# Turning the tails of the attention outputs: fp32 products and a split behind them, or a split ahead and fp16 products

## The chip, the cores and the metric

The kernel runs on one core of a Trainium2 chip. The metric is the device time of one execution in microseconds. One execution was recorded by the hardware profiler; times of the profile are counted from its first instruction. The engines are TensorE (PE, with its weight loads PEld), VectorE (DVE), ScalarE (ACT), GpSimd (POOL) and SyncE (SP, which here issues all DMAs).

## The reference, cut to what matters

```python
# q, k, v: (8 batches, 8 heads, 1152, 64), float32
q_pool = q.reshape(B, H, S // 2, 2, D).mean(axis=3)             # 576 query rows
scores = 1 / sqrt(D) * matmul(q_pool, k.transpose(0, 1, 3, 2))
attn = softmax(scores, axis=-1)
x = matmul(attn, v)  ->  (8, 576, 512), heads side by side
# gated unit
h = maximum(x @ w_in, 0);  u, v = h[..., :512], h[..., 512:]
v_n = (v - mean) / sqrt(var + 1e-6)                             # over the 512 columns
v_s = einsum('ts,bsd->btd', w_spatial, v_n) + b_spatial[None, :, None]
out = (u * v_s) @ w_out
```

All of it is wanted in float32. The kernel reaches that with fp16 products by splitting an operand into two fp16 parts, head and rest, and adding three of the four partial products.

## The kernel before, in words

The work is cut into 32 head pairs i (8 batches of 4 pairs; a pair is two heads in one 128-partition tile). `attention(i)` runs 18 steps, 2 heads by 9 chunks of 128 keys. Each step makes a tile of scores for 512 query rows (L1076, L1077, in a bank `pss`, three of them), takes the exponential on ACT (L1082, tile `pt`), splits it on POOL (L1102) and multiplies it with the split values (L977, L983, L988, into the bank `o`). The query rows number 576 per head, so 64 are left over, the *tail*. The tails of the two heads are done together: scores L1089 and L1093, exponential L1098, and `tail_values(i)` (L1046 to L1048), whose result, divided by its sum, L1052 writes to the tile `xt`. `xt` is [128, 4, 128] fp32, one 128-column block for each pair of a batch; a block holds 64x64 of head 0 and 64x64 of head 1 on its diagonal, and zeros.

While `attention(i)` runs, `maxima(i + 1)` takes the maxima of the scores of the next pair, which the exponentials need: 27 matmuls (L869, L854) and 27 reductions on DVE (L875, tile `mt`), followed by `shift` (L897 to L902), which turns the maxima and carries them to the query rows by DMA. The pair after that is prepared in the same time (`prep`, with a small matmul for the q and k scales, L469).

`turn_main(i)` runs some steps after the last values of a pair, thus within `attention(i + 1)`. It turns the pair's result (`xm`, written by L996) so that the 128 columns of the two heads lie on the partitions, split in two fp16 parts, in the tile `xg` from which the gated unit reads. For batches 0 and 1 (`i < EARLY`) that is done by PE (L1022) and a split behind it (`x_split`: ACT L943, DVE L944). From batch 2 on `turn_by_dma` splits first, into the tile `xc` (ACT L1006, POOL L1007; one buffer), and turns each half by a DMA transpose (L1009, issued by SP).

With the last pair of a batch (i = 3, 7, ..., 31: eight times) `turn_main` also turns the tails of the batch's four pairs: four fp32 products of a 128x128 block of `xt` with `ident2`, an identity of 64 rows that stands twice, one above the other (L1029). The product's 64 columns collapse the diagonal form. They go to one PSUM bank `pm`, and `x_split` copies them in two fp16 parts into the middle piece of `xg` (256 columns, ACT L943 and DVE L944).

After every second batch a gated unit (`gated_unit`, eight pairs' worth of rows) is started. Its steps run interleaved with the attention of the following batches, the last unit alone at the end. Its first part multiplies nine tiles of 128 rows with `w_in` (L1163): four of the first batch's main rows, the fifth of both batches' tails, and four of the second batch's main rows. The other parts are L1230, L1274/L1275 and L1317; the output goes out at L1327. Its PSUM banks are `pw` (two); the last unit also uses the `pss` banks.

PSUM tiles of one name are used in the order in which the program asks for them. `pm` (two buffers) serves the maxima, the shifts, the scales, the tail products and the turn of the tails.

The order of the instructions on each engine is written down by a planner (`class Order`, method `pin`). It simulates the program with a cost for every instruction (`cost`). On each engine it takes, among the instructions whose operands are due, the one that is first in the program. An operand made by another engine can get a margin on top (`SLACK`, in ns) before its reader counts as due:

```python
SLACK = {("Pool", "PE"): 1400, ("Activation", "PE"): 300, ("DVE", "PE"): 400, ("SP", "PE"): 2000,
         ("SP", "Activation"): 3000, ("SP", "DVE"): 3000, ("SP", "Pool"): 3000}
```

The pair is (maker, reader); SP stands for its DMAs. Two rules for tiles with few buffers are part of the plan (method `edges`): the first user of a tile waits for all users of the tile that had its buffer before, and does not begin before the first user of the tile of the same name asked for just ahead of it:

```python
if n is not None and k and (tag, k - 1) in of:
    begun[n].add(users[of[tag, k - 1]][0])
if n is not None and (tag, k - bufs) in of:
    before[n].update(users[of[tag, k - bufs]])
```

On the chip each engine then runs its instructions in that fixed order.

Of the kernel before, what the change touches and what calls it, by code (L numbers as in the profile page):

```python
# [11 lines left out]
F16 = mybir.dt.float16  # L12
BF16 = mybir.dt.bfloat16
F32 = mybir.dt.float32
# [3 lines left out]
AF = mybir.ActivationFunctionType  # L18
# [357 lines left out]
def attn_sgu_kernel(ctx: ExitStack, tc: tile.TileContext, qT, kT, v, w_in, w_spT, b_sp, w_out, out):  # L376
    nc = tc.nc
    P = 128
    B, NHP, _, D, _, S = qT.shape
# [9 lines left out]
    TAIL = S - MAIN  # L389
# [15 lines left out]
    const = order.pool(ctx.enter_context(tc.tile_pool(name="const", bufs=1)), 1)  # L405
# [3 lines left out]
    wk = order.pool(ctx.enter_context(tc.tile_pool(name="wk", bufs=2)), 2)  # L409
# [13 lines left out]
    ones = const.tile([P, P], BF16, name="ones")  # L423
    nc.vector.memset(ones, 1.0)

    ident2 = const.tile([P, D], F32, name="ident2")
    for h in range(2):
        nc.vector.tensor_copy(out=ident2[h * D : (h + 1) * D], in_=ident[h * D : (h + 1) * D, h * D : (h + 1) * D])

# [4 lines left out]
    xt = const.tile([P, NHP, P], F32, name="xt")  # L434
# [493 lines left out]
    def ends_unit(i):  # L928
        return i % (2 * NHP) == 2 * NHP - 1

    def x_rows(n, e):


        if n not in xs:
            t = mo.tile([P, NT * DH], F32, name="xg", bufs=2).bitcast(F16)
            cut = [0, 2 * NHP * MAIN, 2 * NHP * (MAIN + P), 2 * NHP * S2]
            xs[n] = [
                t[:, a:z].rearrange("p (l k t) -> p l k t", l=2, k=NHP) for a, z in zip(cut, cut[1:])
            ]
        return xs[n][{0: 0, 1: 2, None: 1}[e]]  # L940

    def x_split(xg, ps):
        nc.scalar.activation(xg[:, 0], ps, AF.Copy, bias=0.0, scale=1.0)  # L943
        nc.vector.tensor_sub(xg[:, 1], ps, xg[:, 0])  # L944
# [11 lines left out]
    def values(i, k):  # L956
# [35 lines left out]
        if c == NC - 1:  # L992
            if h == 0:
                st["xm"] = wk.tile([P, 4, P], F32, name="xm", bufs=1)
            r = inverse(o[:, :, D], "den")
            nc.vector.tensor_tensor(  # L996
                out=st["xm"][:, :, h * D : (h + 1) * D], in0=o[:, :, 0:D],
                in1=r.unsqueeze(2).to_broadcast([P, 4, D]), op=ALU.mult,
            )
            if h == 1:  # L1000
                later.append([2, lambda: turn_main(i)])

    def turn_by_dma(xm, n, e, hp):

        xc = wk.tile([P, 2, 4, P], F16, name="xc", bufs=1)
        nc.scalar.activation(xc[:, 0], xm, AF.Copy, bias=0.0, scale=1.0)  # L1006
        nc.gpsimd.tensor_sub(xc[:, 1], xm, xc[:, 0])  # L1007
        for l in range(2):
            nc.sync.dma_start_transpose(  # L1009
                out=x_rows(n, e)[:, l, hp].rearrange("p (t q) -> p t q", q=P),  # L1010
                in_=xc[:, l].rearrange("p t d -> p (t d)"),
            )

    def turn_main(i):

        b, hp = divmod(i, NHP)
        n, e = divmod(b, 2)
        xm = state.pop(i)["xm"]
        if i < EARLY:
            ps = ps_m.tile([P, 512], F32, name="pm")  # L1020
            for t in range(4):
                nc.tensor.transpose(out=ps[:, t * P : (t + 1) * P], in_=xm[:, t], identity=ident)  # L1022
            x_split(x_rows(n, e)[:, :, hp], ps)
        else:
            turn_by_dma(xm, n, e, hp)
        if hp == NHP - 1:
            ps = ps_m.tile([P, 512], F32, name="pm")
            for k in range(NHP):
                nc.tensor.matmul(ps[:, k * D : (k + 1) * D], lhsT=xt[:, k], rhs=ident2, start=True, stop=True)  # L1029
            x_split(  # L1030
                x_rows(n, None)[:, :, :, e * TAIL : (e + 1) * TAIL],
                ps[:, : NHP * TAIL].rearrange("p (k t) -> p k t", t=TAIL),
            )
            if ends_unit(i):
                units.append(gated_unit(n))
# [449 lines left out]
```

## Time and profile before

| what | value |
|---|---|
| three runs, us | 1169.83, 1166.50, 1168.87; median 1168.87 |
| the profiled execution | 1166.47 us, span 1164.7 us from the first to the last instruction |
| granted TensorE clock | 0.998 |
| PE, DVE, ACT, POOL busy, us | 1133.2, 862.6, 889.0, 846.6 |
| L1029, turn of the tails | 64 passes, eight at each of the eight batch ends |
| DMA packets | 89146, 133.18 MB |

How to read the rows: in lists of groups a row has line, engine, operation, out<-in by the program's names, partitions x elements and type, xcount, then busy us, mean ns of one, and the idle time of the engine just before with what ended it. A timeline row has start and duration in us, then the same; x2 means that two like instructions are merged. A row of waits has who waited for whom, total us, times, and the longest. The chain that ended last has start, duration and what; it is followed back from the last instruction through whatever released each step. Rows of stretches have busy us and (instruction count) for each engine, then granted clock, DMA share and GB/s. Ends of matmuls are modelled, so that the duration of one matmul overlaps with the next one; the distance from start to start is what counts in a row of them.

### The profile page before, as it was taken

How to read it: one execution, taken by the hardware profiler on the slowest of the kernel's cores; microseconds unless marked ns; L12 is line 12 of the kernel's file. 1: busy time of each engine (PE TensorE's matmuls, PEld its weight loads, DVE VectorE, ACT ScalarE, POOL GpSimd, SP SyncE). 2: the span in 40 equal slices, each digit the busy share in tenths (PEclk: the TensorE clock that was granted, in tenths of full speed). 3: DMA queues.
4: the chain of work that ended last, by engine and by line, in shares of the span. 5: the costliest groups of instructions: out<-in, count | busy, mean ns of one | idle time of the engine just before them, and what ended most of it. 6: DMA issues, size and time to landing. Idle time of an engine off the chain costs nothing.

```text
span 1164.7 us, 33546 instructions
## 1 busy us (share of the span) xinstructions
PE 1133.2 (97%) x13297; PEld 722.5 (62%) x13297; DVE 862.6 (74%) x2247; ACT 889.0 (76%) x1689; POOL 846.6 (73%) x731
## 2 busy tenths in 40 slices
PE   4899999999999999999999999999999999999998
PEld 1677777776666666666666666666666666665453
DVE  7899999867889878656779677865668677822644
ACT  6897899898878978788777877879777967754433
POOL 3667676788897979988877878988787977883000
PEclk9999999999999999999999999999999999999999
DMA  6675365454542353565413544365432431121002
GB/s 211 185 218 170 102 183 172 120 137 112 172 109 77 106 146 83 146 182 134 128 43 79 162 124 109 103 167 145 111 100 79 128 88 23 35 65 37 1 2 82
DMA packets 89146, 133.18 MB, mean 114 GB/s; under 512 B 39902, under 2 KB 48158, under 8 KB 88988
## 3 DMA queue, kind: packets, MB, share of 16 engines
q1 hardware_dynamic: 88988, 131.04, 40.5%
q8 instruction: 104, 1.70, 0.6%
q14 instruction: 54, 0.44, 0.1%
HBM read 81.20 MB, written 9.44 MB: 78 GB/s over the span
## 4 chain that ended last, share of the span: by engine, by line
PE 84%; DVE 6%; ACT 3%; issue 1%; DMA 0%; POOL 0%; ACTq 0%; DVEq 0%
PE pss L1076 9%; PE pss L1077 9%; PE pm L869 8%; PE pw L1317 7%; PE pw L1274 7%; PE pw L1163 7%; PE pw L1230 6%; PE o L988 5%; PE o L977 5%; PE o L983 5%; PE o L970 2%; DVE mt L875 2%; PE pss L1163 1%; PE pss L1274 1%; PE pm L1046 1%; PE pm L1048 1%
## 5 line engine op out<-in xcount | busy, mean ns | idle before, releaser
L1102 POOL TENSOR_TENSOR pt<-pt 128x512 f16<-128x512 f32 x528 | 578.0, 1110 | 163.2 <-ACT pt L1082 160.1
L1082 ACT ACTIVATE pt<-pss,esc 128x512 f32<-128x512 f32 x576 | 388.9, 692 | 109.6 <-PE pss L1077 96.2
L875 DVE TENSOR_REDUCE mt<-pm 128x1 f32<-128x384 f32 x733 | 387.1, 551 | 107.0 <-PE pm L869 90.4
L1076 PE MATMUL pss<-qhi,khi 128*128 128x512 f16 x576 | 218.8, 380 | 1.9 <-ACT pt L1082 1.5
L1077 PE MATMUL pss<-xq,klo 66*128 66x512 f16 (+1 forms) x576 | 219.2, 381 | 0.0
L869 PE MATMUL pm<-khi,qhi 128*128 128x384 f16 x637 | 193.8, 325 | 3.7 <-DVE mt L875 2.9
L977 PEld LDWEIGHTS <-pt 128*128 128x128 bf16 x2112 | 124.0, 98 | 67.5 <-DVE xm L996 1.6
L988 PE MATMUL o<-vp,pt 128*128 128x65 f16 x2112 | 155.4, 193 | 0.0
L977 PE MATMUL o<-vp,pt 128*128 128x65 f16 x2112 | 154.9, 193 | 0.4 <-DVE xm L996 0.4
L983 PE MATMUL o<-vp,pt 128*128 128x64 f16 x2112 | 154.0, 193 | 0.0
L988 PEld LDWEIGHTS <-pt 128*128 128x128 f16 x2112 | 114.1, 98 | 34.1 <-issue 0.6
L869 PEld LDWEIGHTS <-qhi 128*128 128x128 f16 x756 | 72.9, 100 | 56.5 <-issue 11.0
L983 PEld LDWEIGHTS <-pt 128*128 128x128 bf16 x2112 | 102.4, 98 | 3.3
L1163 PE MATMUL pw<-wi_h,xg 128*128 128x512 f16 x240 | 89.2, 379 | 0.0
L1098 ACT ACTIVATE ptl<-pss,esc 128x256 f32<-128x256 f32 (+1 forms) x128 | 64.5, 504 | 29.2 <-PE pss L1093 27.7
L1102 POOL TENSOR_TENSOR ptl<-ptl 128x1152 f16<-128x1152 f32 x32 | 69.8, 2180 | 21.5 <-ACT ptl L1098 21.5
L1230 PE MATMUL pw<-xg,wi_h 128*128 128x512 f16 (+1 forms) x336 | 81.4, 325 | 0.0
L1274 PE MATMUL pw<-ws_h,vv 128*128 128x512 f16 x216 | 79.1, 379 | 0.0
L1317 PE MATMUL pw<-wo_h,vv 128*128 128x512 f16 x216 | 78.5, 378 | 0.0
L875 DVE TENSOR_REDUCE mt<-pw 128x1 f32<-128x384 f32 x131 | 69.8, 547 | 7.1 <-PE pw L869 6.2
L1077 PEld LDWEIGHTS <-klo 66*128 66x128 f16 (+1 forms) x576 | 56.2, 98 | 27.7 <-issue 7.6
L712 POOL TENSOR_TENSOR vp<-vt,vp 128x576 f16<-128x576 f32 x48 | 59.9, 1250 | 12.9 <-ACT vp L710 12.6
(267 smaller groups left out, 2509.0 us busy)
## 6 DMA issues: line engine op xcount, KB each, us to landing
vt<-in_v_dram SPq DMA_DIRECT2D x56, 576.0 KB
qt<-in_qT_dram SPq DMA_DIRECT2D x32, 576.0 KB
kt<-in_kT_dram SPq DMA_DIRECT2D x32, 576.0 KB
khi<-kn SPq DMA_DIRECT2D x128, 144.0 KB
out_dram<-row SPq DMA_DIRECT2D x24, 256.0 KB
qhi<-xq SPq DMA_DIRECT2D x62, 72.0 KB
klo<-klo SPq DMA_DIRECT2D x31, 144.0 KB
u<-in_w_in_dram SPq DMA_DIRECT2D x3, 1024.0 KB
```

Source lines behind the costliest of these rows:

```text
L869: nc.tensor.matmul(pm[:, :W], lhsT=q[:, c0 : c0 + P], rhs=k[:, n * NB : (n + 1) * NB, :], start=True, stop=True,)
L875: nc.vector.reduce_max(out=mt[:, t, n : n + 1], in_=pm[:, :W], axis=AX.X)
L977: nc.tensor.matmul(o[:, t], lhsT=top[:, cols], rhs=vp[:, D : D + D1], start=c == 0 and t == 0, stop=False, skip_group_check=True,)
L983: nc.tensor.matmul(o[:, t, 0:D], lhsT=top[:, cols], rhs=vp[:, 0:D], start=False, stop=False, skip_group_check=True)
L988: nc.tensor.matmul(o[:, t], lhsT=rst[:, cols], rhs=vp[:, D : D + D1], start=False, stop=c == NC - 1, skip_group_check=True,)
L1076: nc.tensor.matmul(o, lhsT=khh[:, h, c, :], rhs=qhl[:, h, q], start=True, stop=False)
L1077: nc.tensor.matmul(o, lhsT=KL[0:rows, h, c, :], rhs=X[0:rows, h, q], start=False, stop=True)
L1082: nc.scalar.activation(pt, ps, AF.Exp, bias=0.0, scale=esc)
L1102: nc.gpsimd.tensor_sub(t.bitcast(F16)[..., 0::2], t, t.bitcast(BF16)[..., 1::2])
L1163: nc.tensor.matmul(ph, lhsT=rows(xa, cc, c0, c0 + P), rhs=wa[:, cc, DH:DF], start=n == 0, stop=n == 3 * NCC - 1,)
L1274: nc.tensor.matmul(pv, lhsT=l, rhs=r[:, 0:MAIN], **fl)
L1317: nc.tensor.matmul(py, lhsT=ga[:, fc, c0 : c0 + P], rhs=wa[:, fc, :], start=m == 0, stop=m == end - 1)
```

## The change

The tails are split before they are turned, as `turn_by_dma` does with the main part, and turned by eight fp16 products (four blocks, two parts) into one full PSUM bank. One copy on ACT then writes both parts to `xg`. The tile for the split has the name `xc` and thus shares the one buffer that `turn_by_dma` uses. `ident2` becomes fp16. The planner is the same and plans the changed program anew.

```diff
-    ident2 = const.tile([P, D], F32, name="ident2")
+    ident2 = const.tile([P, D], F16, name="ident2")
...
         if hp == NHP - 1:
+            xc = wk.tile([P, 2, NHP, P], F16, name="xc", bufs=1)
+            nc.scalar.activation(xc[:, 0], xt, AF.Copy, bias=0.0, scale=1.0)
+            nc.gpsimd.tensor_sub(xc[:, 1], xt, xc[:, 0])
             ps = ps_m.tile([P, 512], F32, name="pm")
-            for k in range(NHP):
-                nc.tensor.matmul(ps[:, k * D : (k + 1) * D], lhsT=xt[:, k], rhs=ident2, start=True, stop=True)
-            x_split(
+            for k in range(2 * NHP):
+                nc.tensor.matmul(
+                    ps[:, k * TAIL : (k + 1) * TAIL], lhsT=xc[:, k // NHP, k % NHP], rhs=ident2, start=True, stop=True
+                )
+            nc.scalar.activation(
                 x_rows(n, None)[:, :, :, e * TAIL : (e + 1) * TAIL],
-                ps[:, : NHP * TAIL].rearrange("p (k t) -> p k t", t=TAIL),
+                ps.rearrange("p (l k t) -> p l k t", l=2, t=TAIL), AF.Copy, bias=0.0, scale=1.0,
             )
```

## The prediction

> **What bounds the kernel now.** The page first: who is busy, and what the chain that ended last consists of.
>
> ```profile
> span 1164.7 us, 33546 instructions
> ...
> PE 1133.2 (97%) x13297; PEld 722.5 (62%) x13297; DVE 862.6 (74%) x2247; ACT 889.0 (76%) x1689; POOL 846.6 (73%) x731
> ...
> PE 84%; DVE 6%; ACT 3%; issue 1%; DMA 0%; POOL 0%; ACTq 0%; DVEq 0%
> ...
> L983 PE MATMUL o<-vp,pt 128*128 128x64 f16 x2112 | 154.0, 193 | 0.0
> ```
>
> TensorE (PE) is busy 97% of the span and is 84% of the chain. A share over the whole span can hide a stage with another limit, so next comes the table of stretches: the start, batches 0 and 1, batches 2 to 7, and the gated unit that runs alone at the end.
>
> ```profile
> 60.00:264.00 204.00, 199.50 (x2479) 147.42 (x2478) 182.60 (x474) 182.07 (x354) 145.05 (x116) 1.00 0.55 159
> 264.00:1062.00 798.00, 793.97 (x9859) 503.62 (x9858) 582.21 (x1542) 625.63 (x1185) 671.25 (x579) 1.00 0.40 108
> 1062.00:1165.00 103.00, 98.92 (x608) 48.16 (x607) 50.78 (x120) 37.42 (x72) 1.17 (x2) 0.99 0.09 29
> ```
>
> The columns are PE, PEld, DVE, ACT, POOL, granted clock, DMA share and GB/s. From 264 to 1062 us PE is idle for 4 of 798 us; POOL stands at 84%, ACT at 78%, DVE at 73%. The waits of PE in that stretch are few; first and last of the four rows:
>
> ```profile
> PE pm L897 <- DVE wide L893: 1.8, 3, 0.8
> ...
> PE pm L469 <- DVE mt L875: 0.2, 1, 0.2
> ```
>
> All four together are 3.7 us, of 24 head pairs. So in this stretch time is the sum of PE's work, and a microsecond of matmul taken away is a microsecond of span, as long as PE finds other work ready wherever the change moves something.
>
> **What the change takes from PE.** Today's turn of the tails is four fp32 products of 64 columns, in the trace eight passes each time:
>
> ```profile
> L1029 PE MATMUL pm<-ident,xt x64: 217/275/318, 146.8 to 1062.0; 128*128 128x64 f32 x64
> ```
>
> The duration of a pass overlaps with the next, so the price is read from the chain, where each piece runs to the next one's end. All eight turns lie on it (the first is split around another line):
>
> ```profile
> 146.96 0.17 PE pm L1029 x2
> ...
> 147.46 0.62 PE pm L1029 x6
> ...
> 148.20 0.12 PE o L983 x4
> ```
>
> ```profile
> 251.16 0.84 PE pm L1029 x8
> ...
> 396.66 0.94 PE pm L1029 x8
> ...
> 525.16 0.84 PE pm L1029 x8
> ...
> 664.98 0.84 PE pm L1029 x8
> ...
> 797.62 0.84 PE pm L1029 x8
> ...
> 937.65 0.84 PE pm L1029 x8
> ...
> 1061.36 0.92 PE pm L1029 x8
> ```
>
> 0.79 + 0.84 + 0.94 + 4 x 0.84 + 0.92 = 6.85 us in all. The new turn is eight fp16 products of 64 columns with 128x128 weights. The trace has that very shape: L983, four in 0.12 us, 30 ns each. Eight cost 0.24 us, the eight turns 1.92 us. The weights of L983 are every second half-word of a tile and the new ones lie side by side, which gives no reason for a higher price. The bounds are 30 ns (L983) and 105 ns (no faster than a pass now, 0.84 / 8); I take 30, since type and shape agree. **Direct gain: 6.85 - 1.92 = 4.93 us**, all of it on the chain.
>
> **What it adds elsewhere.**
>
> ```profile
> L1007 POOL TENSOR_TENSOR xc<-xm,xc 128x512 f16<-128x512 f32 x24 | 30.1, 1256 | 9.4 <-ACT xc L1006 9.1
> ...
> L1006 ACT ACTIVATE xc<-xm 128x512 f16<-128x512 f32 x24 | 15.3, 637 | 4.3 <-DVE xm L996 4.3
> ...
> L943 ACT ACTIVATE xg<-pm 128x512 f16<-128x512 f32 x8 | 4.9, 608 | 0.0
> L944 DVE TENSOR_TENSOR xg<-pm,xg 128x256 f16<-128x256 f32 x8 | 3.3, 417 | 10.9 <-ACT xg L943 10.8
> L943 ACT ACTIVATE xg<-pm 128x256 f16<-128x256 f32 x8 | 3.1, 391 | 1.4 <-PE pm L1029 1.4
> ```
>
> The split before the turn has the shape of the one in `turn_by_dma`: 0.64 us on ACT and 1.26 us on POOL. The copy out of PSUM grows from 256 to 512 columns, 0.39 to 0.61 us, and the subtraction on DVE, 0.42 us, goes. Over eight turns ACT gains 8 x (0.64 + 0.22) = 6.9 us of work, POOL 10.1 us, DVE loses 3.3 us. In the long stretch ACT has 172 us free and POOL 127 us, so the work itself costs nothing; without that cover it would be up to 10 us. The fp16 identity is one cast at the start instead of an fp32 copy: nothing, give or take 0.1 us. No DMA is added or moved.
>
> **What it makes wait.** The new tile has the name `xc` and one buffer, which from batch 2 on the DMA transposes of the same head pair have just been reading. Today's turn of i = 15, beside its main part:
>
> ```profile
> 524.39 0.42 DVE L996 TENSOR_TENSOR xm<-o,den 128x256 f32<-128x256 f32 x1
> ...
> 525.50 0.65 ACT L1006 ACTIVATE xc<-xm 128x512 f16<-128x512 f32 x1
> ...
> 526.18 3.81 SPq L1009 DMA_TRANSPOSE xg<-xc  x2
> ...
> 526.69 0.40 ACT L943 ACTIVATE xg<-pm 128x256 f16<-128x256 f32 x1
> 526.77 1.15 POOL L1007 TENSOR_TENSOR xc<-xm,xc 128x512 f16<-128x512 f32 x1
> ...
> 527.12 0.42 DVE L944 TENSOR_TENSOR xg<-pm,xg 128x256 f16<-128x256 f32 x1
> ```
>
> Today the tail goes at 525.0, beside all this. After the change it comes behind it. When the transposes have landed shows in the DMA busy digits of 1064 to 1070 us (0.15 us each) beside their issue for i = 31:
>
> ```profile
> DMA  0000008999700000049996100079994000000000
> ```
>
> ```profile
> 1065.40 2.51 SPq L1009 DMA_TRANSPOSE xg<-xc  x2
> ```
>
> The last packets end near 1068.65, 0.74 us behind the second issue. For i = 15 that makes 529.99 + 0.74 = 530.7. Then come ACT 0.64 and POOL 1.26: 532.6 at the earliest, and with the planner's margins (3.0 us from a DMA to ACT, 1.4 us from POOL to PE) about 537. So the turn slips by 8 to 12 us. Its PSUM tile `pm` is handed out in program order, and every later `pm` must begin behind it: the row maxima of the next pair but one, the q and k scales, the shifts and the tail products. At the ends of batches 2 to 6 (i = 11, 15, 19, 23, 27) a hole of 8 to 12 us opens in that stream; batches 0 and 1 have no transposes, and behind i = 31 no maxima follow. What the hole displaces, by the reductions of the maxima:
>
> ```profile
> 525.00:537.00 12.00, 6.25 (x13) 1.00 0.50 130
> 537.00:549.70 12.70, 5.80 (x12) 1.00 0.69 172
> 549.70:555.00 5.30, 0.16 (x1) 1.00 0.15 20
> ```
>
> ```profile
> 526.00:537.00 11.00, 11.00 (x138) 6.79 (x136) 7.71 (x22) 9.25 (x21) 9.37 (x9) 1.00 0.54 141
> 537.00:555.00 18.00, 18.00 (x215) 11.28 (x213) 11.14 (x31) 14.00 (x26) 15.73 (x14) 1.00 0.53 127
> ```
>
> Up to 13 reductions (6.25 us of DVE) move into 537 to 555, where DVE has 18.0 - 11.1 = 6.9 us free. They just fit if DVE runs full; otherwise the next pair starts 1 to 3 us late. PE loses up to 13 matmuls in the hole and gets them back later. Meanwhile the scores and values of the current pair and the gated unit are ready: the unit's first four tiles need nothing of the late tail. That is the cover, and PE's idle time of 4 us in 798 speaks for it. Without cover the price is the late start, up to 3 us a hole, 15 us in all. I take 0.2 us a hole, somewhat over the 3.7 us / 24 = 0.15 us that a pair waits on DVE now, **1.0 us in all**.
>
> For the last unit the turn of i = 31 ends near 1068.65 + 0.64 + 1.26 + 0.24 + 0.61 = 1071.4 plus margins. Its fifth product tile is the first to read it, behind this row:
>
> ```profile
> 1066.00 7.77 PE pss L1163 x36
> ```
>
> That is 1073.8, and the margins shift the order rather than stop PE, since tiles behind it sit in other banks. Nothing is charged.
>
> **Sum.** -4.93 + 1.0 = -3.9 us. The profiled execution took 1166.47 us, 1.8 us over its span, and would become 1162.6 us. The three runs have the median 1168.87, 2.4 us above that execution; on the median the forecast is 1168.87 - 3.9 = **1165.0 us**, 0.33% faster. A measurement of this kernel can tell about 0.3%, 3.5 us, from no change, so the forecast lies close to that bound.
>
> **Rivals.** *The holes eat the gain.* Everything works, but catching up is dearer than 0.2 us: from 0.3 to 1.6 us a hole, sum -3.4 to +3.1 us, 1165.4 to 1172.0. For it: DVE must run full behind each hole, PE's order is fixed ahead, and its few waits are on DVE already. Against: PE is never short of work now. 36%.
>
> *ACT stands before the transposes.* The copy into `xc` is queued on ACT at a fixed place. If the transposes land later than the planner allows, ACT stands there, and behind it the exponentials (L1082) on which PE's score banks and POOL's splits wait. If ACT stood from today's place of the tail copy (526.7) to the landing (530.7), that is 4 us, five times 20 us; half of it reaching PE gives -4.93 + 10 = +5 us, all of it +15: 1174 to 1184 us. It decides once a landing is more than 3 us behind plan. For it: the transposes share queues with large loads (DMA share 0.54 here). Against: the planner's 3 us. 12%. [...]
>
> *The small products cost more.* At twice the price of L983, 60 ns apiece, eight turns take 3.8 us, the gain is 3.0 us, with the holes 2.0: 1166.9 us. Against it stand the 2112 matmuls of L983 at 30 ns. 4%. [...]
>
> **How the numbers follow.** The forecast has 48%, the rivals 36, 12 and 4%. Forecast alone: from the direct gain less 1.4 us for the draw of the runs (the shown ones lie 2.4 below to 1.0 above their median), 1168.87 - 4.93 - 1.4 = 1162.5, up to 1165.4. The range reaches over the second case to 1172.0 and leaves out the 12% of the third. Faster by over 0.3%: 0.48; within 0.3%: 0.36 + 0.04 = 0.40; slower: 0.12.
>
> **What would show it.** Right: 64 fp16 matmuls of the turn, eight in 0.24 us on the chain; ACT copies of 0.64 and POOL subtractions near 1.2 us on `xc`, 32 instead of 24; the turn 8 to 12 us later at i = 11 to 27, with no reduction of maxima in that time; PE still within 5 us of busy in the long stretch, and the gated unit's matmuls in the holes. Wrong: PE waits on `xc`, on `mt` or on the shifts of more than a microsecond a hole; waits of ACT on a transpose; eight products in over 0.4 us. The forecast fails if PE's idle time between 264 and 1062 us grows by over 2 us, or if no hole appears and the gain is whole.

## The result and the profile after

The changed kernel takes 1175.38 us (median of four runs, 1174.03 to 1176.07) against 1169.34 us before in the same runs: ratio 1.0057, 95% interval 1.0042 to 1.0071. It is slower by about 6 us; the forecast was 3.9 us faster. The profiled execution took 1175.37 us with a span of 1173.6 us, 8.9 us over that of before, whose profiled execution was the fastest of its four: some 3 us of the 8.9 are the draw. All medians below are of executions at a granted clock of 0.99 or more; three at 0.66 to 0.77 (1455 to 2120 us) are left out. The page after, lines as before:

```profile
span 1173.6 us, 33541 instructions
...
PE 1131.6 (96%) x13297; PEld 717.4 (61%) x13297; DVE 864.5 (74%) x2239; ACT 893.9 (76%) x1697; POOL 847.7 (72%) x739
...
PE 79%; DVE 9%; ACT 3%; issue 1%; DMA 1%; POOL 1%; SPq 0%; ACTq 0%; DVEq 0%; POOLq 0%
```

PE's share of the chain fell from 84 to 79%, DVE's rose from 6 to 9%: PE now waits more. The new turn itself is what was forecast. The first row gives it by its line, the second is from the chain behind i = 15, four products in 0.12 us, 30 ns each:

```profile
L1032 PE MATMUL pm<-ident,xc x64: 190/193/193, 148.0 to 1084.0; 128*128 128x64 f16 x64
```

```profile
541.46 0.12 PE pm L1032 x4
```

The turn comes as late as was forecast. The timeline of i = 15, SP and the split beside the main turn:

```profile
530.77 0.41 DVE L996 TENSOR_TENSOR xm<-o,den 128x256 f32<-128x256 f32 x1
...
532.87 3.38 SPq L1009 DMA_TRANSPOSE xg<-xc  x2
533.43 1.16 POOL L1007 TENSOR_TENSOR xc<-xm,xc 128x512 f16<-128x512 f32 x1
...
540.26 0.62 ACT L1028 ACTIVATE xc<-xt 128x512 f16<-128x512 f32 x1
...
541.30 0.28 PE L1032 MATMUL pm<-ident,xc 128*128 128x64 f16 x4
...
541.79 1.17 POOL L1029 TENSOR_TENSOR xc<-xt,xc 128x512 f16<-128x512 f32 x1
```

The second transpose was issued by 536.25, landed near 537.0 (with the 0.74 us of the prediction), and ACT comes to the tails 3.3 us behind that, which fits the planner's margin of 3 us (no run changed the margin). The first four products need the head alone, so the `pm` tile begins at 541.30, 10.1 us behind `xm`. In that time the reductions of the maxima all but stop (stretches of the tile `mt`, DVE busy and count), at i = 15, 19, 23 and 27:

```profile
531.00:542.00 11.00, 1.24 (x3) 1.00 0.48 135
671.00:682.00 11.00, 0.56 (x1) 1.00 0.52 134
806.00:817.00 11.00, 1.34 (x3) 1.00 0.47 136
946.00:956.00 10.00, 0.56 (x1) 1.00 0.33 87
```

Behind i = 11 the pause is shorter: there are still eight reductions (3.86 us) from 394 to 407 us. Inside the four holes PE has enough to do, here all engines in the first of them (PE, PEld, DVE, ACT, POOL):

```profile
531.00:542.00 11.00, 11.00 (x137) 6.54 (x135) 2.22 (x6) 9.78 (x21) 11.00 (x11) 1.00 0.48 135
```

So the time is lost outside the holes. PE by stretches, before and after (length, then busy; the difference is idle):

```profile
140.00:264.00 124.00, 122.95 (x1538) 1.00 0.54 159
264.00:520.00 256.00, 253.60 (x3137) 1.00 0.47 125
520.00:1060.00 540.00, 538.37 (x6694) 1.00 0.37 99
```

```profile
140.00:264.00 124.00, 120.38 (x1518) 1.00 0.50 149
264.00:520.00 256.00, 249.65 (x3094) 1.00 0.45 122
520.00:1060.00 540.00, 534.44 (x6649) 1.00 0.38 102
```

Idle time of PE grew from 1.05, 2.40 and 1.63 us to 3.62, 6.35 and 5.56 us, 10.5 us in all. The modelled end of a matmul (a product of 64 columns shows 193 ns where the next one starts after 30 ns) hides the first 0.16 us of every gap, so this counts short. Counted instead from start to start of the matmuls, each distance less the lowest quarter's distance for that shape before, PE's work fell by 5.3 us and its idle time rose by some 14 us; the difference is the 8.9 us of span. What PE waits for from 264 to 1071 us, the three largest rows (total us, times, longest):

```profile
PE pm L897 <- DVE wide L893: 4.6, 5, 1.9
PE pw L1322 <- DVE vv L496: 4.2, 6, 1.5
PE pm L469 <- DVE mt L875: 1.3, 1, 1.3
```

Before, all such rows came to 3.7 us and the second was not among them. L1322 is the last product of the gated unit, L496 the split of its factor on DVE. In the list of ACT's waits no transpose appears.

### The profile page after: what moved, and what is told of

It reads as the page before. It is cut to its first block, busy times and chain, and to the rows that moved or that the text cites. A ratio compares the mean times of both kernels' runs of the same rounds, so it can differ in the third digit from the quotient of the medians.

```text
span 1173.6 us, 33541 instructions
## 1 busy us (share of the span) xinstructions
PE 1131.6 (96%) x13297; PEld 717.4 (61%) x13297; DVE 864.5 (74%) x2239; ACT 893.9 (76%) x1697; POOL 847.7 (72%) x739
## 4 chain that ended last, share of the span: by engine, by line
PE 79%; DVE 9%; ACT 3%; issue 1%; DMA 1%; POOL 1%; SPq 0%; ACTq 0%; DVEq 0%; POOLq 0%
PE pss L1082 8%; PE pss L1081 8%; PE pm L869 8%; PE pw L1279 7%; PE pw L1168 7%; PE pw L1235 6%; PE pw L1322 6%; PE o L977 5%; PE o L988 5%; PE o L983 4%; DVE mt L875 3%; PE o L970 1%; DVE vv L496 1%; PE pss L1168 1%; PE pss L1279 1%; PE pss L1322 1%
## 5 line engine op out<-in xcount | busy, mean ns | idle before, releaser
L1107 POOL TENSOR_TENSOR pt<-pt 128x512 f16<-128x512 f32 x528 | 571.8, 1100 | 161.2 <-ACT pt L1087 157.8
L1087 ACT ACTIVATE pt<-pss,esc 128x512 f32<-128x512 f32 x576 | 389.3, 692 | 136.0 <-PE pss L1082 125.2
L1322 PE MATMUL pw<-wo_h,vv 128*128 128x512 f16 x216 | 79.0, 379 | 4.4 <-DVE vv L496 4.2
L826 POOL TENSOR_TENSOR klo<-kt,kn 128x640 f16<-128x640 f32 (+1 forms) x48 | 62.0, 1297 | 17.1 <-ACT kn L825 12.9
```

Of the source, the lines that this page charges most:

```text
L1087: nc.scalar.activation(pt, ps, AF.Exp, bias=0.0, scale=esc)
L1107: nc.gpsimd.tensor_sub(t.bitcast(F16)[..., 0::2], t, t.bitcast(BF16)[..., 1::2])
L1322: nc.tensor.matmul(py, lhsT=ga[:, fc, c0 : c0 + P], rhs=wa[:, fc, :], start=m == 0, stop=m == end - 1)
```

## The experiments

In all runs "before" is the kernel before on the same chip in the same runs; its medians lay between 1168.33 and 1169.06 us. The groups of runs were on different chips.

### Is it the wait for the transposes? Four runs

The wait alone: the kernel before, with a copy between (from batch 2 on).

```diff
+            src = xt
+            if i >= EARLY:
+                src = wk.tile([P, 2, NHP, P], F16, name="xc", bufs=1)...bitcast(F32)
+                nc.scalar.activation(src, xt, AF.Copy, bias=0.0, scale=1.0)
             for k in range(NHP):
-                nc.tensor.matmul(..., lhsT=xt[:, k], rhs=ident2, ...)
+                nc.tensor.matmul(..., lhsT=src[:, k], rhs=ident2, ...)
```

> The kernel before, with its fp32 products and its split behind them, but from batch 2 on the products read a copy of the tails that ACT puts into the buffer of xc; so the turn has to wait for the DMA transposes, and nothing else is gained or added but 0.64 us of ACT at six batch ends. Theory A (the late turn holds back every later pm tile, the holes cost PE time): the change lost 9.3 - 3.4 = 5.9 us of span between the starts of pair 8 and the end although six turns saved 3.7 us, so the holes cost about 9.6 us: 1178 to 1180 us, holes of 9 to 12 us in the reductions of the maxima behind i = 11, 15, 19, 23, 27. Theory B (the added ACT and POOL work and a worse plan cost the time, the wait is hidden): within 2 us of before, 1168 to 1171 us.

Measured: 1175.96 us, ratio 1.0071 (1.0058 to 1.0085), 7.6 us slower. Without any change to products or split the wait costs more than the whole change. That is theory A, at four fifths of the 9.6 us expected and 2 us under the range.

The turn first: the block of the tails stands ahead of the main turn from batch 2 on.

```diff
+        if hp == NHP - 1 and i >= EARLY:
+            tail()        # the changed block, as it is
         if i < EARLY: ...
         else:
             turn_by_dma(xm, n, e, hp)
+        if hp == NHP - 1 and i < EARLY:
+            tail()
```

> The changed kernel, but from batch 2 on the split and turn of the tails stand ahead of the main part's turn in the program, so the shared buffer is taken before the transposes read it; same operations, same shapes. Theory A: no holes in the maxima, the 9.6 us are gone and the loss of the first two batches (3.4 us) stays: 1165 to 1168 us. Theory B: as the changed kernel, 1174 to 1177 us.

Measured: 1170.61 us, ratio 1.0019 (1.0011 to 1.0028). Same operations, another order, 5 us less, and from 520 us on PE idles no more than before (busy for 538.36 of 540 us). But the time is 2.6 us over the range and still slower than before: there is a second loss, larger than the 3.4 us allowed for.

The bank of the gated unit for the turn:

```diff
-            ps = ps_m.tile([P, 512], F32, name="pm")
+            ps = ps_w.tile([P, 512], F32, name="pw")
```

> The changed kernel, but the turn's PSUM tile is a pw (the gated unit's) instead of a pm; the turn slips behind the transposes as before. Theory A, and the pm order as its way: no holes in the maxima, the gated unit's banks wait instead; PE has the attention as other work, so 1167 to 1172 us. If the slip itself or theory B is what costs: 1174 to 1177 us or more.

Measured: 1169.84 us, ratio 1.0015 (1.0003 to 1.0027). The turn slips as before (10.1 us behind `xm` at i = 15) and still most of the loss is gone. But it went in one stretch: PE's idle time from 264 to 520 us fell from 6.35 to 0.76 us. From 520 to 1060 us, with four of the five slips, 4.4 of 5.6 us are left, now in other waits, 1.1 us of them of the turn itself for its split:

```profile
264.00:520.00 256.00, 255.24 (x3170) 1.00 0.47 127
520.00:1060.00 540.00, 535.59 (x6678) 1.00 0.37 99
```

So a slip costs with either bank, and this run does not show that the order of the `pm` tiles is its only way. The bank is changed in batches 0 and 1 too, which the next section shows to lose time of their own in that first stretch.

Another buffer for the split:

```diff
+            if i < EARLY: xc = ... name="xc"
+            else:         xc = wk.tile([P, DH], F32, name="row").bitcast(F16)...
```

> The changed kernel, but from batch 2 on the split goes to a buffer named row (two, the gated unit's) instead of xc; the turn does not wait for the transposes, but for the gated unit's rows. Theory A: holes of at most 3 us, 1165 to 1170 us. Theory B: 1174 to 1177 us.

Measured: 1171.09 us, ratio 1.0023 (1.0014 to 1.0032). 1.1 us over the range, on the same side as with the turn first: the wait goes, the second loss stays.

### Which batches lose? Five runs

Batches 0 and 1 alone, batches 2 to 7 alone: the changed block under `if i < EARLY:` or `if i >= EARLY:`, and the old block, with an fp32 identity `ident3` of its own, in the other case.

> Only the tails of batches 0 and 1 are split first and turned by fp16 products; from batch 2 on the fp32 products and the split behind them stand. In these two batches no DMA transposes are in the way. Theory A, with the loss of the first 250 us as a second, separate thing (ACT and DVE are over 90% busy there and ACT gets 0.9 us more for each turn): pair 8 starts 3 us late and that stays, 1170 to 1172 us. If the early loss comes from the later holes or is chance: 1167 to 1169 us.

Measured: 1175.03 us, ratio 1.0060 (1.0039 to 1.0081). Two turns without any transposes in the way cost 6.2 us, where 1.2 to 3.2 were expected. PE by stretches in this run:

```profile
140.00:264.00 124.00, 121.41 (x1533) 1.00 0.51 151
264.00:520.00 256.00, 248.82 (x3054) 0.99 0.44 119
520.00:1060.00 540.00, 538.37 (x6689) 1.00 0.38 104
```

Idle time is up by 1.5 us in the first stretch and by 4.8 us in the second, where not one changed instruction stands, and not at all in the third. What the second stretch adds lies in two places, here in this run and then in the kernel before (all engines):

```profile
340.00:360.00 20.00, 17.43 (x209) 11.51 (x207) 17.60 (x38) 12.39 (x24) 12.73 (x12) 0.93 0.40 106
455.00:480.00 25.00, 21.34 (x289) 13.60 (x287) 21.11 (x50) 20.77 (x38) 21.53 (x18) 1.00 0.32 86
```

```profile
340.00:360.00 20.00, 18.81 (x224) 11.97 (x223) 18.52 (x43) 14.41 (x27) 13.99 (x12) 1.00 0.28 73
455.00:480.00 25.00, 25.00 (x305) 15.70 (x302) 20.98 (x49) 23.79 (x45) 22.28 (x19) 1.00 0.27 76
```

From 340 to 360 us PE waits for the shift (1.9 us) and the maxima (0.6 us), from 455 to 480 us for the split of the gated unit's factor:

```profile
PE pw L1334 <- DVE vv L499: 3.3, 2, 1.7
```

> Only the tails of batches 2 to 7 are changed (shared buffer, turn behind the transposes); batches 0 and 1 keep fp32 products. Theory A: the holes are all there, the early loss is not: before plus 9.6 us for the holes less 3.7 us for six turns, 1173 to 1176 us. If the early loss is the greater part of the damage: under 1171 us.

Measured: 1171.84 us, ratio 1.0025 (1.0011 to 1.0038), just below the range; a second run of it 1171.87 us and 1.0023 (1.0014 to 1.0032).

> The run with the change in batches 2 to 7 alone once more, for a profile (the first one's execution took 2120 us at a clock of 0.77 and shows nothing). Theory A: 1170 to 1174 us, the start of pair 8 within 1 us of before, holes of 9 to 12 us in the reductions of the maxima behind i = 11, 15, 19, 23, 27, and PE's loss behind them, not before pair 12.

```profile
140.00:264.00 124.00, 122.95 (x1541) 1.00 0.53 153
264.00:520.00 256.00, 252.10 (x3112) 1.00 0.44 122
520.00:1060.00 540.00, 536.44 (x6660) 1.00 0.38 103
```

Nothing is lost up to 264 us; 1.5 us more idle than before in the second and 1.9 us more in the third stretch, by this view that leaves out the first 0.16 us of each gap; by the distances of the starts it is 7.1 us more from 264 us on.

Batches 2 to 7 with the turn first (the two edits above together):

> Batches 0 and 1 keep fp32 products; from batch 2 on the change with split and turn ahead of the main part's turn, so without the wait for the transposes. Theory A: no holes, no early loss, each of the six turns gives its 0.6 us: 1164 to 1166 us, faster than before and after. If an unexplained loss around pairs 12 to 16 (about 3.5 us in the run with the turn put first) is caused by the new turns and not by the late start of these pairs: 1167 to 1169 us.

```profile
140.00:264.00 124.00, 122.94 (x1537) 1.00 0.54 159
264.00:520.00 256.00, 253.80 (x3149) 1.00 0.46 126
520.00:1060.00 540.00, 538.37 (x6735) 1.00 0.37 99
```

Measured: 1164.19 us, ratio 0.9959 (0.9947 to 0.9971): faster than before. Idle time is that of before in every stretch, and the span of 1161.1 us is 3.6 us shorter, six turns at 0.6 us. The unexplained loss between pairs 12 and 16 is not there. Against the runs with the shared buffer's wait (1171.84 and 1171.87) that is 7.7 us for five holes, 1.5 us a hole.

A split that needs neither `xc` nor more of ACT:

```diff
+            top, rst = xt.bitcast(BF16)[:, :, 1::2], xt.bitcast(F16)[:, :, 0::2]
+            nc.gpsimd.tensor_sub(rst, xt, top)
             for k in range(NHP):
-                nc.tensor.matmul(..., lhsT=xt[:, k], rhs=ident2, start=True, stop=True)
+                for n_, x in enumerate((top, rst)):
+                    nc.tensor.matmul(..., lhsT=x[:, k], rhs=ident2, start=n_ == 0, stop=n_ == 1)
             x_split(...)   # as before
```

> All eight turns by fp16-rate products, but the tails are split in place on POOL alone into a bf16 top half and an fp16 rest, eight products are accumulated in pairs, and the split behind them stays as before; no use of xc, no more ACT work, DVE's subtraction stays. The parts have fewer bits than two fp16 parts. Theory A: no wait for transposes, no holes, no added ACT work in batches 0 and 1: the direct gain of 4.9 us less up to 1.5 us, 1163.5 to 1165 us. If the new plan as such costs time: 1168 us or more.

Measured: 1163.35 us, ratio 0.9958 (0.9945 to 0.9971). The first two stretches:

```profile
140.00:264.00 124.00, 120.17 (x1524) 1.00 0.51 151
264.00:520.00 256.00, 254.59 (x3152) 1.00 0.47 127
```

PE's idle time in the first rose nevertheless, to 3.8 us, although ACT has no more to do than before; in the second it fell to 1.4 us. So the idle time of the first stretch needs no added work of ACT, and a shift there can also turn out well later on.

### What is the early loss? Eight runs

Two tiny edits to the kernel before and one with the work alone; in the program they stand at the turns of batches 0 and 1:

```diff
             if i < EARLY:
+                nud = sm.tile([P, 1], F32, name="nud", bufs=2)
+                nc.scalar.activation(nud, xt[:, 0, 0:1], AF.Copy, bias=0.0, scale=1.0)   # nudge_act
+                nc.vector.tensor_copy(out=nud, in_=xt[:, 0, 0:1])                        # or nudge_dve
```

> The kernel before, and at the turns of batches 0 and 1 one more ACT copy of a single column of the tails into a tile that nothing reads, about 0.2 us of work twice. If the early loss is the price of the work that the change adds there, or of its later turn: within 1.5 us of before, 1167 to 1170 us. If the order of the first 250 us is so tightly packed that any edit shifts the plan and the stretch of 340 to 390 us, where DVE is over 90% busy, multiplies the shift: 2 to 6 us off before, in either direction.

> The same with one column copied by DVE in place of ACT, twice 0.15 us. Same two readings: within 1.5 us of before, or 2 to 6 us off it, and then not by the same amount as the ACT copy.

```diff
             if i < EARLY:
+                xc = wk.tile([P, 2, NHP, P], F16, name="xc", bufs=1)
+                nc.scalar.activation(xc[:, 0], xt, AF.Copy, bias=0.0, scale=1.0)
+                nc.gpsimd.tensor_sub(xc[:, 1], xt, xc[:, 0])      # read by nothing
```

> The kernel before with its fp32 products and the split behind them; at the turns of batches 0 and 1 ACT and POOL split the tails into xc as the change does, but nothing reads the parts. So the added work is there without the changed products and without the longer way to them. If the added work on ACT and POOL makes the early loss: 1173 to 1177 us, as the run with the change in batches 0 and 1 alone (1175 us). If the longer way through POOL to the products makes it: 1167 to 1170 us.

Measured: the copy on ACT 1168.96 us, 1.0003 (0.9992 to 1.0014); the copy on DVE 1170.09 us, 1.0014 (1.0004 to 1.0023); the split that nothing reads 1170.52 us, 1.0016 (1.0006 to 1.0026). The first stretch of the DVE copy:

```profile
140.00:264.00 124.00, 121.41 (x1522) 1.00 0.54 157
```

Two copies of one column, by estimate 0.3 us of DVE work together (the one-column L949 and L950 took 156 and 154 ns before), make PE idle 1.5 us more, as much as the change in batches 0 and 1 alone (121.41 as well). The split that nothing reads does the same, 2.5 us short of the 1173 that would have put the whole early loss on the added work:

```profile
140.00:264.00 124.00, 121.24 (x1513) 1.00 0.52 153
```

So this part, some 1.5 us, needs neither the changed products nor a later turn: the plan of these batches moves when little is put in. The copy on ACT (the one-column L727 took 297 ns before, so by estimate 0.6 us for the two) left it alone, but it says less than it seems. A copy of one column of `xt` is due as soon as that column is written, and the planner placed the two on ACT at 87 and 168 us, the two on DVE at 150 and 206 us, while the turns come at 147 and 251 us. The 4.8 us of the second stretch appear in none of the three runs.

The plan of the run with batches 0 and 1 alone, shifted once more at pair 8:

```diff
+        if i == EARLY:
+            nud = sm.tile([P, 1], F32, name="nud", bufs=2)
+            nc.vector.tensor_copy(out=nud, in_=xt[:, 0, 0:1])
```

> The change in batches 0 and 1 alone, and one further copy of a single column by DVE (0.15 us) at the main turn of pair 8, near 285 us, read by nothing. If the 7 us between pairs 11 and 15 are the luck of one plan: the loss there falls to under 3 us, 1169 to 1172 us in all. If they follow from the change in batches 0 and 1 itself: 1174 to 1177 us as without the copy.

Measured: 1173.74 us, 1.0047 (1.0035 to 1.0059), between the two readings. 5.0 of the 6.2 us stay, so the loss is not the accident of one plan; but what the second stretch adds to PE's idle time is halved, from 4.8 to 2.5 us (busy for 251.09 of 256 us), so its size is in part.

Four copies of the gated unit off DVE, with the change in batches 0 and 1 alone and in the kernel before:

```diff
-                nc.vector.tensor_copy(out=te[0:TAIL, 0, :], in_=h[0:TAIL])    # and three more
+                nc.scalar.activation(te[0:TAIL, 0, :], h[0:TAIL], AF.Copy, bias=0.0, scale=1.0)
```

> The change in batches 0 and 1 alone, and the four copies into te (about 2 us of DVE near 350 us, where PE waits 2.1 us on DVE) are made by ACT. If the crowded DVE of 330 to 390 us makes the 7 us: most of them go, 1169 to 1172 us. If not: 1174 to 1177 us.

> The kernel before with the four copies into te on ACT, as the control for the run above: DVE is no bound there outside the crowded stretch, so within 1.5 us of before, 1167 to 1170 us. A plan shifted by it could move 2 us either way.

Measured: with the change in batches 0 and 1 1167.14 us, 0.9988 (0.9978 to 0.9998); without it 1164.77 us, 0.9966 (0.9953 to 0.9979). The control was off: it gains 4.0 us by itself; PE's idle time from 264 to 1060 us falls from 4.0 to 0.9 us. The distance of the two is 2.4 us, against 6.2 us with the copies on DVE. The second stretch with the change and without it:

```profile
264.00:520.00 256.00, 253.62 (x3138) 1.00 0.47 126
```

```profile
264.00:520.00 256.00, 255.29 (x3158) 1.00 0.47 129
```

There 1.7 us of idle time is left of the 4.8. By this pair the crowded DVE near 350 us would make about three fifths of the early loss.

The parts together, without the change in batches 0 and 1 and with it (turn first from batch 2 on, te copies on ACT):

> fp32 products in batches 0 and 1, from batch 2 on the change with the tails' turn ahead of the main part's, and the four te copies on ACT. If the parts add up: 1168.7 - 4.8 (turn first, late) - 3.8 (te on ACT) = 1160 us, 1159 to 1162. If both gains are of the same waits near 350 us: 1162.5 to 1165 us.

> The change in all batches, from batch 2 on with the tails' turn ahead, and the te copies on ACT. If DVE's crowded stretch made the larger part of the early loss: 1 to 3 us above the run with fp32 products in batches 0 and 1, 1161 to 1164 us. If it did not: 6 us above it, 1166 us.

Measured: 1162.20 us, 0.9945 (0.9927 to 0.9962), and 1166.77 us, 0.9978 (0.9968 to 0.9988). The first is the fastest kernel of the case, 6.9 us under before, but some 2 us short of the full sum: in the second stretch the te copies take 1.7 us of idle time from the kernel before and 0.3 us from the one with the turn first; why is not shown. The distance of the two is 4.6 us, neither the 1 to 3 us nor the 6 us expected. With the holes gone and DVE relieved, the turns of batches 0 and 1 still lose more than their 1.2 us of gain.

All five comparisons with and without the change in batches 0 and 1 together, PE's added idle time in us:

| with the change, against without | te copies on | 140 to 264 | 264 to 520 |
|---|---|---|---|
| batches 0 and 1 alone, against before | DVE | 1.5 | 4.8 |
| the same with one more copy at pair 8, against before | DVE | 1.8 | 2.5 |
| all batches, turn first, against batches 2 to 7, turn first | DVE | 1.7 | 2.4 |
| batches 0 and 1 alone, against before | ACT | 2.1 | 1.7 |
| all batches, turn first, against batches 2 to 7, turn first | ACT | 1.9 | 1.4 |

The first stretch loses about the same in all of them. The second loses 2.4 to 4.8 us with the te copies on DVE and 1.4 to 1.7 us with them on ACT. So DVE's crowd is a part of it, and how large a part depends on the rest of the plan.

## Why the prediction was wrong, point by point

**The direct gain** was right: 30 ns a product, 0.6 us a turn. It shows bare in the run with batches 2 to 7 and the turn first, 3.6 us of span for six turns with PE's idle time unchanged.

**The slip and the holes** were right: 10.1 us behind `xm` at i = 15, ACT's copy 3.3 us behind the landing as the margin of 3 us has it, the reductions all but gone for that time at four of the five batch ends and thinned out at the fifth, i = 11.

**The cover inside the hole** was right: PE is busy for 11.00 of 11.00 us, and for 12.52 of 13.00 behind i = 11.

**The price of a hole** is the first step that failed: "I take 0.2 us a hole ... 1.0 us in all". The runs show 1.5 us a hole, 7.7 us in all, and the wait alone, with no products changed, costs 7.6 us. The prediction closed the account at the end of the same pair: the reductions "just fit", the next pair starts up to 3 us late, and the gated unit covers it. But the maxima are not caught up in one pair. Counted in the run with batches 2 to 7 alone against the one with the turn first, at 430 us, 23 us behind the turn of i = 11, the reductions are 12 us late and the scores 3 us, where both were 1 to 2 us late ahead of that turn; at 520 us it is 8 and 4 us. PE then waits in small pieces, for the maxima and in the gated unit, which was to be the cover. The largest of its waits from 250 us on that are shorter (the first, 1.0 us) or absent with the turn first:

```profile
PE pm L872 <- DVE mt L878: 1.8, 5, 0.5
PE pw L1334 <- DVE vv L499: 1.0, 3, 0.4
PE pss L1093 <- ACT ptl L1115: 0.8, 2, 0.4
```

That the late maxima also make the unit's products wait is read from these waits; no run moved the unit's split to another time. The largest single piece of the changed kernel is 455 to 480 us, where the unit's products wait for the split on DVE (1.8 us) and the late preparation of a pair waits for the maxima (1.3 us). All engines there, in the changed kernel and then with batches 2 to 7 alone:

```profile
455.00:480.00 25.00, 21.96 (x255) 12.87 (x252) 21.82 (x44) 21.87 (x40) 19.61 (x17) 1.00 0.22 50
```

```profile
455.00:480.00 25.00, 24.13 (x297) 14.50 (x295) 19.91 (x49) 22.47 (x41) 21.06 (x18) 1.00 0.27 79
```

The hole behind i = 11 alone leaves PE idle for 0.9 us there. The change in batches 0 and 1 alone, without any hole, leaves it idle for 3.7 us. So this piece belongs more to the step that follows. The rival "the holes eat the gain" named up to 1.6 us a hole; its price was right, and it should have been the forecast for the holes. Its upper end, 1172.0 us, still falls short of the measured time by what batches 0 and 1 lose.

**Batches 0 and 1** are the second step that failed: "all of it on the chain", with no price beside it. For the added work the prediction took the cover of the long stretch ("the work itself costs nothing"), but two of the eight turns stand before it. The change there alone costs 6.2 us, with a gain of 1.2 us in it, and the added split alone, which nothing reads, 1.9 us. The row of 60 to 264 us in the prediction showed why that could be: DVE 182.60 and ACT 182.07 of 204 us beside PE at 199.50, three engines near their limit. A copy of one column brings 1.5 us of idle PE there. The rest comes later: near 350 us, where DVE is about 90% busy, PE waits for the shift and the maxima, and from 455 to 480 us for the split of the unit's factor on DVE. That DVE's crowd near 350 us has a part in it is shown by the te copies, which lower what the second stretch loses; that it makes most of it is not shown, since the whole loss falls from 6.2 to 2.4 us in one pair of runs and only from about 6.4 to 4.6 us in the other. Why the plan of these batches reacts to some edits and not to others, and by what way a late start there ends as a wait 200 us later, stays open.

The two losses overlap: batches 0 and 1 alone cost 6.2 us and batches 2 to 7 alone 3.1 to 3.3 us, together 6.0 us and not 9.4. One place where they meet is 455 to 480 us.

**The rivals.** ACT before the transposes: no such wait in the list; the margin held. How far work on ACT would have stood behind such a wait was thus not put to the test. The profile after has one short case behind another wait: ACT sat idle for 1.47 us until DVE had made `xm`, the copy L1006 followed at 745.77, and the exponential L1087 began behind it at 746.31, although the last product of its scores had started at 743.59 and shows 0.38 us. Small products at twice the price: the factor of two was an assumption; the chain shows 30 ns a product. The only case that the prediction put above 1172 us had the wrong mechanism: no queue stalled; delayed work met other work later.

## What to carry to other kernels

When a step is made cheaper by sending it through a shared buffer, price the buffer's other users first: 0.6 us saved on the bound engine was paid with 1.5 us, because the tile behind the buffer also comes late, and in this plan a rotating bank hands out its places in program order, so that the users behind it wait. Putting the same code ahead of the other user turned a loss into a gain. In a stage where three engines are over 89% busy, as here up to 264 us, a saving on one of them need not appear (1.2 us saved in batches 0 and 1 came with 6.2 us lost); there an edit is measured, not costed. And cover has to be followed until the delayed work is caught up, not only while the delay lasts. Last, a piece of idle time is put down to a cause only when the run without that cause lacks it: 455 to 480 us looked like the price of a hole and was there without one.

## What the runs showed of the hardware

PE started the turn with the four head products 0.5 us before POOL began the rest (541.30 against 541.79): in this program a matmul waits for the half tile it reads, not for the tile.

The granted clock is not even within an execution. In the profiled one with the change in batches 0 and 1 alone it fell to 0.57 from 357 to 361 us, right behind a wait of PE of 1.9 us (all engines, then the clock):

```profile
355.00:357.00 2.00, 0.31 (x6) 0.32 (x7) 1.94 (x5) 0.41 (x1) 1.28 (x1) 1.00 0.00 0
357.00:361.00 4.00, 4.00 (x38) 2.60 (x36) 2.61 (x9) 4.00 (x11) 1.04 (x1) 0.57 0.11 22
```

A clock of 0.57 over 4 us is 1.7 us of full speed lost. The runs with the turn first and with the other buffer have the same behind the same wait (0.69 and 0.57 from 357 to 361 us); the changed kernel and the run with the copy at pair 8 have the wait and a clock of 1.00. So the wait alone does not decide it, and what does is not shown. In executions that have it, up to 1.7 us of the early loss is clock and not waiting; PE's idle time above does not contain it, as PE counts as busy then (4.00 of 4.00).
